# A fused attention, MoE and FFN kernel: where and in which pieces the FFN's weights are converted from 64 to 32 bits

## The chip, the cores and the metric

The kernel runs on one core of a Trainium2 chip. The metric is the device time of one execution in microseconds (us); the median of three runs is 1493.49 (1490.66 to 1493.54). Engines are named as in the profile: PE (matrix multiply, with its weight loads as PEld), DVE (vector), ACT (activation), POOL (GpSimd), SP (sync). SP, ACT and POOL each have a queue from which they issue DMA transfers; POOL's transfers are among them the indirect ones.

## The reference

```
scores = einsum('bhij,hg->bgij', q @ k^T / sqrt(64), w_pre)       # 4 batches, 12 heads, 448 rows, 64 columns
attn   = einsum('bhij,hg->bgij', softmax(scores), w_post)
x      = (attn @ v) as 1792 tokens x 768
logits = x @ w_gate; e = argmax(logits)                           # 8 experts
x      = softmax(logits)[e] * (relu(x @ w1[e]) @ w2[e])           # w1 768x1024, w2 1024x768
h      = x @ w_in; out = (h * sigmoid(h)) @ w_out                 # w_in 768x2048, w_out 2048x768
```

All inputs but w_in and w_out are 32-bit floats. Those two reach the kernel as 64-bit floats, in `wf`: 16 slices f, each 128 rows of 1536 columns (a slice of w_in beside a slice of w_out). The chip's engines see pairs of 32-bit words (low, high), and the kernel itself makes 32-bit floats of them: `high & 0xfffff`, scaled to a mantissa; `low` added to it; the sign put in; the exponent shifted out of `high`, moved to the 32-bit bias, and multiplied in. That is five DVE and two ACT instructions for a chunk, a load of D (two words a column) before and a store to `w_d[f]` in memory behind. A chunk's working buffer is CM.

## The kernel before

Products in full precision are made of three matmuls on numbers split in a high and a low part (`mm3`, L785): ACT makes the high part (a cast), DVE the low one (a subtraction).

**Attention** (to about 525 us). 16 blocks of 120 or 88 rows, each with 12 or 9 groups of 10 rows by 12 heads. A group is mixed (L787 to L789), its maximum taken (L373), exponentiated on ACT (L383), scaled, mixed again (L414), and evacuated (`a_sb`, L256). A planner (`Plan`, L147) sets the order of every instruction from priorities, costs in us written beside each operation, and rings of buffers; operations that list ACT and DVE both go to the one that it has free. Scores S go from rows to groups by SP's transfers (`relay`, L336). Each block ends with its gate on DVE (L486 to L500, seven instructions on 120x8 numbers and one exponential on ACT). Among this work the planner spreads the conversion (`convert`, L518) of the slices 0 to 3 (`FA = 4`) in 24 chunks of 256 columns.

**MoE** (to about 930 us). Tokens are sorted by expert into 18 slots of 128 rows. POOL's queue gathers a slot's rows (L849) and scatters its results y to `y_d` (L895). Per slot the weights are split (L838, L839), `mm1` makes h (L875) and `mm2` makes y (L893). From the 24th step on `Convert` (L917) converts slices 4 to 7 in 16 chunks of 384 columns: a new chunk's load (L936) and an old one's store (L958) are issued by POOL, and a step of each chunk in work is taken after each quarter slot. In the last slots ACT's queue also loads rows of `y_d` for the FFN (`xload`, L907), which waits for the scatters.

**FFN** (the rest). 80 units (gi, f): five groups of rows (four of 384, one of 256) by 16 slices; the first 40 units take slices 0 to 7 for all groups and store partial sums to `p_d`, the other 40 take slices 8 to 15 and add them. The order is that of the code: `s1` (18 matmuls, sigmoid L985, product L987, split into gh and gl), in some units the transposes of the next group (`fT`), `s2` of the unit before (18 matmuls), `fsplit` of the weights two units ahead (rhi on ACT, rlo on DVE, L844 and L845), `fload` of those four units ahead (SP, L902), and a step of the conversion of slices 8 to 15: 16 chunks of 768 columns, begun over 36 units, two buffers each of D and CM, POOL issuing. In the step k counted from the load: 1 L946, 2 L948 (ACT), 3 L950 and L951, 4 L954 (ACT), 5 L956, L957 and the store.

Of the kernel before, what the change touches and what calls it, by code (L numbers as in the profile page):

```python
# [9 lines left out]
F32 = mybir.dt.float32  # L10
# [9 lines left out]
DM = H * D  # L20
# [8 lines left out]
NS0 = 18  # L29
# [3 lines left out]
FA = 4  # L33
# [50 lines left out]
def fused_kernel(ctx: ExitStack, tc: tile.TileContext, q, k, v, w_pre, w_post, wg, w1, w2, wf, cst, out):  # L84
# [57 lines left out]
    attention(tc, nc, q, k, v, x_d, oh, cum, zsum, c_e8, ident, (wp1h, wp1l), wp2, wg_sb, wf, w_d, bias_e, bias_1)  # L142
# [86 lines left out]
def attention(tc, nc, q, k, v, x_d, oh, cum, zsum, c_e8, ident, wp1, wp2, wg_sb, wf, w_d, bias_e, bias_1):  # L229
    with ExitStack() as st:  # L230
# [16 lines left out]
        T = [tuple(one.tile([128, S], F32R, name=f"{n}{h}") for n in ("kh", "kl")) for h in range(H)]  # L247

# [221 lines left out]
        def lsum(i, part):  # L470
            def fn(e):
                m = blocks[i][2]
                if ("lg", i) not in tiles:
                    tiles["lg", i] = sm.tile([120, 2, E], F32, name="lg", tag="lg", bufs=2)
                V.reduce_sum(tiles["lg", i][:m, part, :], tiles["rows", i, part][:, :, 128:].rearrange("p j e -> p e j"),
                             axis=AX.X)
            return fn
# [8 lines left out]
        def gate(i):  # L486
            def fn(e):
                m = blocks[i][2]
                lgs = tiles.pop(("lg", i))
                mx, nm, mn = (sm.tile([120, 1], F32, name=n, tag=n, bufs=2) for n in ("lmx", "lnm", "lmn"))  # L490
                lg, cand = (sm.tile([120, E], F32, name=n, tag=n, bufs=2) for n in ("lgt", "cand"))
                V.tensor_tensor(out=lg[:m], in0=lgs[:m, 0, :], in1=lgs[:m, 1, :], op=ALU.add)
                V.reduce_max(mx[:m], lg[:m], axis=AX.X)
                V.scalar_tensor_tensor(out=cand[:m], in0=lg[:m], scalar=mx[:m], in1=c_e8[:m],
                                       op0=ALU.is_equal, op1=ALU.mult)
                V.tensor_reduce(out=mn[:m], in_=cand[:m], axis=AX.X, op=ALU.min)
                V.tensor_scalar(out=oh[:m, i, :], in0=c_e8[:m], scalar1=mn[:m], scalar2=None, op0=ALU.is_equal)
                V.tensor_tensor(out=cum[:, i + 1, :], in0=cum[:, i, :], in1=oh[:, i, :], op=ALU.add)
                V.tensor_scalar(out=nm[:m], in0=mx[:m], scalar1=-1.0, scalar2=None, op0=ALU.mult)
                tiles["lx", i] = (lg, nm)  # L500
            return fn

        def gexp(i):
            def fn(e):
                m = blocks[i][2]
                lg, nm = tiles.pop(("lx", i))
                ex = sm.tile([120, E], F32, name="ex", tag="ex", bufs=2)
                A.activation(out=ex[:m], in_=lg[:m], func=ACTF.Exp, bias=nm[:m], accum_out=zsum[:m, i:i + 1])
            return fn
# [94 lines left out]
        for i in range(NBLK):  # L604
# [18 lines left out]
            for half in range(2):  # L623
# [6 lines left out]
                add(("lsum", i, half), n + P["rows"], ((DVE, .18),), lsum(i, half), [("rows", i, half)], [],  # L630
                    [("tp", "rows", i, half)])
            add(("store", i), f, ((SP, .63),), store(i), [("rowsx", i, h) for h in range(2)], extra=3.0)
            add(("gate", i), n + P["rows"], ((DVE, 1.6),), gate(i), [("lsum", i, h) for h in range(2)] + ([("gate", i - 1)] if i else []))
            add(("gexp", i), n + P["rows"], ((ACT, .4),), gexp(i), [("gate", i)])
# [157 lines left out]
def experts(tc, nc, x_d, y_d, w1, w2, wf, w_d, p_d, bias_e, bias_1, out, ident, oh, cum, zsum, consts,  # L792
# [6 lines left out]
    with outer:  # L799
# [117 lines left out]
        class Convert:  # L917


            def __init__(self, pool, f0, f1, cols, steps):  # L920
                self.pool, self.cols = pool, cols
                self.chunks = [(f, c) for f in range(f0, f1) for c in range(0, 2 * DM, cols)]
                self.starts = [n * steps // len(self.chunks) for n in range(len(self.chunks))]
                self.time, self.begun, self.live = 0, 0, []

            def tick(self):
                for x in list(self.live):
                    x[0] += 1
                    self.step(*x)
                    if x[0] == 5:  # L930
                        self.live.remove(x)
                while self.begun < len(self.chunks) and self.starts[self.begun] <= self.time:
                    f, c = self.chunks[self.begun]
                    d = self.pool.tile([128, self.cols, 2], I32, name="D", tag="D", bufs=2)
                    m = self.pool.tile([128, self.cols], I32, name="CM", tag="CM", bufs=2)
                    nc.gpsimd.dma_start(out=d.rearrange("p a b -> p (a b)"), in_=wv[f, :, 2 * c:2 * (c + self.cols)])  # L936
                    self.live.append([0, f, c, d, m])
                    self.begun += 1
                self.time += 1

            def step(self, k, f, c, d, m):
                V, A = nc.vector, nc.scalar
                low, high = d[:, :, 0], d[:, :, 1]
                fl = m.bitcast(F32)
                if k == 1:
# [261 lines left out]
```

## Time and profile before

| | us |
|---|---|
| median of three runs | 1493.49 |
| the profiled execution | 1491.27 |
| its span, first to last instruction | 1489.0 |
| PE, DVE, ACT, POOL busy | 1346.9, 1118.9, 915.4, 144.4 |
| mean granted clock of PE | 0.963 |

Busy time is read with care: matmuls are pipelined, and a PE that is busy by this table need not be at its peak. A row of the stretches below has, in this order: start and end in us, the length, the busy time of PE, PEld, DVE, ACT and POOL (with the number of instructions), PE's granted clock, the share of time that the DMA engines were busy, and GB/s. A timeline's row has start, duration, engine, line, operation, tiles (written <- read), and in brackets the idle time before it and what ended that by the profile.

### The profile page before, as it was taken

To read this page: it belongs to the slowest core of one execution; us is meant where nothing else is said; L and a number is where in the kernel's file an instruction comes from. 1 tells how busy PE (TensorE), PEld (TensorE's weight loads), DVE (VectorE), ACT (ScalarE), POOL (GpSimd) and SP (SyncE) were. 2 spreads that over 40 slices of the span, in tenths; PEclk is the share of its full clock that TensorE was granted. 3 is DMA by queue.
4 is the path that set the end of the run, shared out by engine and by line. 5 is a ranking of instruction groups with operands and counts; after the bars stand their busy time and mean duration, and the time that the engine had idled before them with its cause. 6 is when DMAs were issued, how large, how long until landed. Compare 5 with 4: busy or idle time off the path is not lost. (4 is left out here: it accounts for less than half of the span.)

```text
span 1489.0 us, 23973 instructions
## 1 busy us (share of the span) xinstructions
PE 1346.9 (90%) x8838; PEld 1222.2 (82%) x8838; DVE 1118.9 (75%) x2022; ACT 915.4 (61%) x1574; POOL 144.4 (10%) x161
## 2 busy tenths in 40 slices
PE   4899999999999989999989888979697949999998
PEld 2787887878788878888877777979696949999997
DVE  5999899989999758888988888557475647455554
ACT  4788787868877636778886777535253525333333
POOL 4000000000000020421211211010101010001001
PEclk9999999999999989999999999989798979999999
DMA  8346545554543360594648642556556546355543
GB/s 242 137 153 174 190 141 161 172 157 149 176 158 130 76 219 22 199 382 147 217 159 306 217 141 80 190 169 212 191 169 202 183 167 223 128 191 191 176 143 138
DMA packets 105417, 259.83 MB, mean 174 GB/s; under 512 B 8956, under 2 KB 61472, under 8 KB 105296
## 3 DMA queue, kind: packets, MB, share of 16 engines
q1 hardware_dynamic: 92096, 200.57, 40.5%
q0 software_dynamic: 11184, 52.18, 10.3%
q10 hardware_dynamic: 2016, 5.51, 1.1%
q8 instruction: 72, 1.18, 0.3%
q14 instruction: 49, 0.40, 0.1%
HBM read 254.28 MB, written 36.18 MB: 195 GB/s over the span
## 5 line engine op out<-in xcount | busy, mean ns | idle before, releaser
L839 DVE TENSOR_TENSOR rlo<-wraw,rhi 128x1536 fp32r<-128x1536 f32 x144 | 246.7, 1755 | 44.8 <-ACT rhi L838 44.5
L838 ACT CAST rhi<-wraw 128x1536 fp32r<-128x1536 f32 x144 | 205.1, 1476 | 11.3 <-DMA wraw<-in_moe_w_dram 11.3
L845 DVE TENSOR_TENSOR rlo<-wf,rhi 128x1536 fp32r<-128x1536 f32 x80 | 140.5, 1758 | 67.8 <-ACT rhi L844 67.8
L414 PEld LDWEIGHTS m<-WM,E 120*112 120x112 f32 (+1 forms) x1440 | 168.5, 177 | 24.8 <-issue 6.3
L414 PE MATMUL m<-WM,E 120*112 120x120 f32 (+1 forms) x1440 | 178.0, 268 | 9.4 <-DVE WM L403 7.5
L787 PE MATMUL b<-fxhi,rhi 128*128 128x384 f32 (+1 forms) x480 | 160.9, 335 | 26.8 <-DVE sg L987 23.4
L787 PE MATMUL b<-rhi,gh 128*128 128x384 f32 x436 | 153.0, 351 | 24.7 <-ACT gh L844 23.9
L789 PE MATMUL b<-fxhi,rlo 128*128 128x384 f32 (+1 forms) x480 | 159.4, 332 | 1.4 <-DVE rlo L845 1.4
L788 PE MATMUL b<-fxlo,rhi 128*128 128x384 f32 (+1 forms) x480 | 159.3, 332 | 0.0
L789 PE MATMUL b<-rhi,gl 128*128 128x384 f32 x436 | 150.7, 346 | 0.0
L788 PE MATMUL b<-rlo,gh 128*128 128x384 f32 x436 | 150.7, 346 | 0.0
L985 ACT ACTIVATE sg<-b 128x384 f32<-128x384 f32 (+1 forms) x80 | 37.5, 469 | 164.4 <-PE b L789 164.1
L844 ACT CAST gh<-sg 128x384 fp32r<-128x384 f32 (+1 forms) x77 | 38.1, 495 | 154.8 <-DVE sg L987 154.8
L383 ACT ACTIVATE E<-m,mx 120x448 f32<-120x448 f32 x180 | 113.9, 634 | 24.8 <-DVE mx L373 13.1
L844 ACT CAST rhi<-wf 128x1536 fp32r<-128x1536 f32 x80 | 118.1, 1478 | 3.5 <-issue 2.2
L787 PEld LDWEIGHTS b<-fxhi,rhi 128*128 128x128 f32 x480 | 93.5, 195 | 29.4 <-DVE sg L987 25.6
L373 DVE TENSOR_REDUCE mx<-m 120x1 f32<-120x448 f32 x180 | 110.4, 617 | 4.2 <-PE m L789 2.8
L357 DVE TENSOR_TENSOR GL<-G,GH 120x448 fp32r<-120x448 f32 x180 | 109.8, 616 | 0.3
L787 PEld LDWEIGHTS b<-rhi,gh 128*128 128x128 f32 x436 | 84.9, 195 | 26.2 <-ACT gh L844 24.8
L323 PE MATMUL qkp<-kh,qs 128*120 128x448 f32 (+1 forms) x192 | 83.6, 436 | 23.3 <-DVE qs L314 20.4
L256 ACT CAST GH<-G 120x448 fp32r<-120x448 f32 (+1 forms) x151 | 85.1, 565 | 31.5 <-PE m L789 14.3
L789 PE MATMUL b<-rhi,hlo 128*128 128x384 f32 x288 | 97.7, 339 | 1.7 <-DVE hlo L845 1.7
(192 smaller groups left out, 3092.7 us busy)
## 6 DMA issues: line engine op xcount, KB each, us to landing
wraw<-in_moe_w_dram SPq DMA_DIRECT2D x76, 1536.0 KB
wf<-w_d SPq DMA_DIRECT2D x80, 768.0 KB
G<-S SPq DMA_DIRECT2D x176, 210.0 KB
D<-in_wf_dram POOLq DMA_DIRECT2D x16, 768.0 KB, 5.6
rawq<-in_q_dram SPq DMA_DIRECT2D x32, 360.0 KB
raw<-in_k_dram SPq DMA_DIRECT2D x36, 224.0 KB
D<-in_wf_dram SPq DMA_DIRECT2D x24, 256.0 KB
D<-in_wf_dram POOLq DMA_DIRECT2D x16, 384.0 KB, 3.6
```

Of the source, the lines that this page charges most:

```text
L256: (A.copy if eng == "act" else V.tensor_copy)(out, in_)
L357: V.tensor_tensor(out=t[:n], in0=x[:n], in1=hi[:n].bitcast(F32), op=ALU.subtract)
L373: V.tensor_reduce(out=mx[:n], in_=tiles["m1", i, g][:n, :S], axis=AX.X, op=ALU.max, negate=True)
L383: A.activation(out=t[:n], in_=tiles.pop(("m1", i, g))[:n, :S], func=ACTF.Exp, bias=tiles.pop(("mx", i, g))[:n], accum_out=tiles["z", i, g ...
L414: nc.tensor.matmul(p[:, c, :, :nr], x[:n, c * CH:(c + 1) * CH], wm[:n, :, :nr], start=True, stop=True)
L787: nc.tensor.matmul(p, lh, rh, start=first, stop=False)
L788: nc.tensor.matmul(p, lh, rl, start=False, stop=False)
L789: nc.tensor.matmul(p, ll, rh, start=False, stop=last)
L838: nc.scalar.copy(hi, src)
L839: nc.vector.tensor_tensor(out=lo, in0=src, in1=hi.bitcast(F32), op=ALU.subtract)
L844: nc.scalar.copy(hi, src)
L845: nc.vector.tensor_tensor(out=lo, in0=src, in1=hi.bitcast(F32), op=ALU.subtract)
```

## The change

Slices 0 to 7 are converted in the attention (48 chunks of 256 columns), none in the MoE, and 8 to 15 in the FFN in 24 chunks of 512 columns. There a chunk has three buffers of D and CM, a tile CE for the exponent, its steps in units 2 to 5 after its load, and SP issues the load ahead of the unit's `fload`. The gates of four blocks are computed together, from sums kept in `lgs`; the logits have their maximum subtracted on DVE, and the exponentials are summed there. A copy of the partial sums goes from DVE to ACT.

```
-FA = 4
+        lgs = one.tile([120, 4, 2, E], F32, name="lgs")
         def lsum(i, part):
-                V.reduce_sum(tiles["lg", i][:m, part, :], ...)
+                V.reduce_sum(lgs[:m, i % 4, part, :], ...)
-        def gate(i):            # 7 DVE instructions on [120, 8], each block
+        def gate(b):
+                V.tensor_tensor(out=lg, in0=lgs[:, :, 0, :], in1=lgs[:, :, 1, :], op=ALU.add)
+                V.tensor_reduce(out=mx, in_=lg, axis=AX.X, op=ALU.max)
+                V.tensor_tensor(out=lg, in0=lg, in1=wide(mx), op=ALU.subtract)
+                V.scalar_tensor_tensor(out=cand, in0=lg, scalar=0.0, in1=ce, op0=ALU.is_equal, op1=ALU.mult)
+                V.tensor_reduce(out=mn, in_=cand, axis=AX.X, op=ALU.min)
+                V.tensor_tensor(out=cand, in0=ce, in1=wide(mn), op=ALU.is_equal)
+                V.tensor_tensor(out=oh[:, w], in0=cand, in1=wide(c_val[:120, w]), op=ALU.mult)
+                for i in range(4 * b, 4 * b + 4):
+                    V.tensor_tensor(out=cum[:, i + 1, :], in0=cum[:, i, :], in1=oh[:, i, :], op=ALU.add)
+        def gexp(b):  ...  A.activation(out=tiles["ex", b], in_=tiles.pop(("lx", b)), func=ACTF.Exp)
+        def zadd(b):  ...  V.reduce_sum(zsum[:, 4 * b:4 * b + 4], tiles.pop(("ex", b)), axis=AX.X)
-        for f in range(FA):
+        for f in range(FH):
-        class Convert: ...
+        CC = 512
+        chunks = [(f, c) for f in range(FH, NF) for c in range(0, 2 * DM, CC)]
+        def conv_load(n, steps):
+            while len(live) < len(chunks) and len(live) * steps // len(chunks) <= n:
+                d = gpool.tile([128, CC, 2], I32, name="D", tag="D", bufs=3)
+                nc.sync.dma_start(out=d.rearrange("p a b -> p (a b)"), in_=wv[f, :, 2 * c:2 * (c + CC)])
+                live.append([n, f, c, d, None, None])
+        def conv_step(n):
+                if k == 2:
+                    m = x[4] = gpool.tile([128, CC], I32, name="CM", tag="CM", bufs=3)
+                    e = x[5] = gpool.tile([128, CC], I32, name="CE", tag="CE")
+                    V.tensor_scalar(out=m, in0=high, scalar1=0xfffff, ...)
+                    V.tensor_scalar(out=e, in0=high, scalar1=20, scalar2=0x7ff, ...)
+                elif k == 3:            # ACT: mantissa of m, exponent of e
+                elif k == 4:            # DVE: low added, sign put in (the last reads of D)
+                elif k == 5:
+                    V.tensor_tensor(out=fl, in0=fl, in1=e.bitcast(F32), op=ALU.mult)
+                    nc.gpsimd.dma_start(out=w_d[f][:, c:c + CC], in_=fl)
-                        nc.vector.tensor_copy(ob[:, 384:], acc[2 * j + 1][:, :384])
+                        nc.scalar.copy(ob[:, 384:], acc[2 * j + 1][:, :384])
-            conv = Convert(wr, FA, FH, 384, 4 * NS0 - 30)
-            slots(0, NS0, hook, tick)
+            slots(0, NS0, hook)
-            conv = Convert(gpool, FH, NF, DM, len(work) // 2 - 4)
+                conv_load(n, len(work) // 2 - 4)
                 if n + 4 < len(work):
                     fload(n + 4)
-                conv.tick()
+                conv_step(n)
```

DVE in the FFN from the end of unit 5 (units counted from 0), before; the number behind CM and D tells chunks apart:

```order
L845 TENSOR_TENSOR rlo_11910<-wf_11793,rhi_11909 128x1536
L956 TENSOR_TENSOR CM_11612<-CM_11612,D_11611 128x768
L957 SCALAR_TENSOR_TENSOR CM_11612<-D_11611,CM_11612 128x768
L950 SCALAR_TENSOR_TENSOR CM_11737<-D_11736,CM_11737 128x768
L951 TENSOR_SCALAR D_11736<-D_11736 128x768
L946 TENSOR_SCALAR CM_11857<-D_11856 128x768
L987 TENSOR_TENSOR sg_11940<-b1_11921,sg_11940 128x384
L845 TENSOR_TENSOR gl_11944<-sg_11940,gh_11943 128x384
L845 TENSOR_TENSOR fxlo1_11641<-b0_11947,fxhi1_11640 128x3x128
```

The same place after (L956 is the multiplication now, L944 and L945 the AND and the shift, L986 the sigmoid product):

```order
L852 TENSOR_TENSOR rlo_11838<-wf_11717,rhi_11837 128x1536
L956 TENSOR_TENSOR CM_11657<-CM_11657,CE_11658 128x512
L952 SCALAR_TENSOR_TENSOR CM_11721<-D_11597,CM_11721 128x512
L953 SCALAR_TENSOR_TENSOR CM_11721<-D_11597,CM_11721 128x512
L944 TENSOR_SCALAR CM_11847<-D_11715 128x512
L945 TENSOR_SCALAR CE_11848<-D_11715 128x512
L986 TENSOR_TENSOR sg_11870<-b1_11851,sg_11870 128x384
L852 TENSOR_TENSOR gl_11874<-sg_11870,gh_11873 128x384
L852 TENSOR_TENSOR fxlo1_11562<-b0_11877,fxhi1_11561 128x3x128
L852 TENSOR_TENSOR rlo_11902<-wf_11781,rhi_11901 128x1536
L956 TENSOR_TENSOR CM_11721<-CM_11721,CE_11722 128x512
L944 TENSOR_SCALAR CM_11913<-D_11779 128x512
```

Before, the first step of chunk CM_11857 stands directly behind the last steps of CM_11612, whose buffer it takes, and ahead of the next sigmoid product. After, CM_11847 has a buffer of its own, and that of CM_11657 is first written again, as CM_11913, one unit later than its multiplication.

POOL's queue in the middle of the MoE, before:

```order
L895 DMA y_d_61<-y_9182,idx_s_102 1792x768
L936 DMA D_9342<-in_wf_dram 128x768
L849 DMA xg_9345<-x_d_60,idx_g_101 128x768
L958 DMA w_d5_67<-CM_9180 128x384
L936 DMA D_9428<-in_wf_dram 128x768
L895 DMA y_d_61<-y_9379,idx_s_102 1792x768
L849 DMA xg_9544<-x_d_60,idx_g_101 128x768
L958 DMA w_d5_67<-CM_9343 128x384
L936 DMA D_9581<-in_wf_dram 128x768
L958 DMA w_d5_67<-CM_9429 128x384
L895 DMA y_d_61<-y_9584,idx_s_102 1792x768
```

and after (L856 is the gather, L902 the scatter):

```order
L902 DMA y_d_61<-y_8105,idx_s_102 1792x768
L856 DMA xg_8257<-x_d_60,idx_g_101 128x768
L902 DMA y_d_61<-y_8289,idx_s_102 1792x768
L856 DMA xg_8469<-x_d_60,idx_g_101 128x768
L902 DMA y_d_61<-y_8501,idx_s_102 1792x768
L856 DMA xg_8653<-x_d_60,idx_g_101 128x768
L902 DMA y_d_61<-y_8685,idx_s_102 1792x768
L856 DMA xg_8837<-x_d_60,idx_g_101 128x768
```

The conversion's loads and stores, which stood between scatters and gathers, are gone.

SP's queue in the first half of the FFN, before:

```order
L902 DMA wf_12355<-w_d0_62 128x1536
L902 DMA wf_12414<-w_d1_63 128x1536
L902 DMA wf_12475<-w_d2_64 128x1536
L902 DMA wf_12537<-w_d3_65 128x1536
L902 DMA wf_12604<-w_d4_66 128x1536
L902 DMA wf_12674<-w_d5_67 128x1536
```

and after (L909 is the weights' load):

```order
L909 DMA wf_11717<-w_d7_69 128x1536
L932 DMA D_11779<-in_wf_dram 128x1024
L909 DMA wf_11781<-w_d0_62 128x1536
L909 DMA wf_11841<-w_d1_63 128x1536
L932 DMA D_11905<-in_wf_dram 128x1024
L909 DMA wf_11907<-w_d2_64 128x1536
L932 DMA D_11971<-in_wf_dram 128x1024
L909 DMA wf_11973<-w_d3_65 128x1536
L909 DMA wf_12039<-w_d4_66 128x1536
```

Loads of D now stand between the loads of the weights, two for every three.

Over the whole attention the planner's order gives DVE 53 copies of a_sb instead of 64, 59 of S instead of 65, 41 casts instead of 44, and 31 copies of xT and xb instead of 26; ACT has the others.

## Rows read from the trace of the kernel before

**Rows 1.** Five stretches: busy PE, PEld, DVE, ACT, POOL, then clock, DMA.
```profile
100.00:500.00 400.00, 383.60 (x3315) 328.39 (x3313) 373.24 (x1022) 313.89 (x751) 0.00 (x0) 1.00 0.50 158
660.00:765.00 105.00, 100.19 (x527) 88.39 (x526) 95.39 (x95) 88.94 (x102) 23.54 (x24) 1.00 0.58 195
765.00:930.00 165.00, 142.93 (x716) 123.96 (x715) 135.76 (x141) 118.85 (x137) 28.79 (x32) 0.94 0.53 184
930.00:1249.00 319.00, 264.33 (x1464) 258.84 (x1464) 186.99 (x234) 133.15 (x186) 24.36 (x44) 0.90 0.55 185
1249.00:1489.00 240.00, 233.08 (x1386) 232.27 (x1384) 124.61 (x149) 92.14 (x121) 17.20 (x16) 1.00 0.48 169
```
**Rows 2.** DVE's waits, 930 to 1249 us: in total, times, longest.
```profile
DVE CM L946 <- DMA w_d<-CM: 51.3, 8, 10.8
...
DVE CM L946 <- DMA D<-in_wf_dram: 6.9, 6, 1.3
```
**Rows 3.** PE's waits in the same stretch.
```profile
PE b L787 <- ACT gh L844: 23.9, 4, 12.9
PE b L787 <- DVE sg L987: 23.4, 5, 10.0
```
**Rows 4.** Timeline of DVE in one unit of that stretch.
```profile
1116.18 0.56 DVE L987 TENSOR_TENSOR sg<-b,sg 128x384 f32<-128x384 f32 x1 [0.34 <-ACT sg L985]
1117.32 0.56 DVE L845 TENSOR_TENSOR gl<-sg,gh 128x384 fp32r<-128x384 f32 x1 [0.58 <-ACT gh L844]
1119.18 1.76 DVE L845 TENSOR_TENSOR rlo<-wf,rhi 128x1536 fp32r<-128x1536 f32 x1 [1.30 <-ACT rhi L844]
...
1129.57 0.56 DVE L946 TENSOR_SCALAR CM<-D 128x768 int32<-128x768 int32 x1 [5.30 <-DMA w_d<-CM]
```
**Rows 5.** Groups by form there: busy us, mean ns, idle before.
```profile
L950 DVE SCALAR_TENSOR_TENSOR CM<-D,CM 128x768 f32<-128x768 uint32 x16 | 15.2, 951 | 0.0
L951 DVE TENSOR_SCALAR D<-D 128x768 int32<-128x768 int32 x16 | 9.0, 561 | 0.6
```
**Rows 6.** Timeline of DVE in the attention, 271 to 279 us.
```profile
271.62 0.29 DVE L532 TENSOR_SCALAR CM<-D 128x256 int32<-128x256 int32 x1
271.82 0.65 DVE L256 COPY a_sb<-m 112x480 f32<-112x480 f32 x1
...
276.31 0.41 DVE L538 SCALAR_TENSOR_TENSOR CM<-D,CM 128x256 int32<-128x256 int32 x1
276.63 0.28 DVE L403 TENSOR_SCALAR WM<-wp,rz 120x120 f32<-120x120 f32 x1
...
277.63 0.14 DVE L492 TENSOR_TENSOR lgt<-lg 120x8 f32<-120x8 f32 x1
...
278.88 0.27 DVE L403 TENSOR_SCALAR WM<-wp,rz 120x120 f32<-120x120 f32 x1
```
**Rows 7.** A group of ACT in the attention, by form.
```profile
L534 ACT ACTIVATE CM<-CM,bias 128x256 f32<-128x256 int32 x19 | 9.6, 507 | 0.7 <-DVE CM L532 0.6
```
**Rows 8.** Timeline of ACT late in the MoE.
```profile
778.41 0.56 ACT L893 ACTIVATE y<-b,gate_s 128x384 f32<-128x384 f32 x1
...
790.00 0.34 ACTq L907 DMA_DIRECT2D x<-y_d  x1
790.39 0.60 ACT L875 ACTIVATE h<-b 128x512 f32<-128x512 f32 x1 [8.20 <-PE b L788]
```
**Rows 9.** Timeline of POOL at the same time.
```profile
783.48 0.55 POOL L958 DMA_DIRECT2D w_d<-CM  x1 [12.43 <-DVE CM L957]
784.33 1.42 POOL L895 DMA_INDIRECT y_d<-y,idx_s  x1 [0.30 <-issue]
```
**Rows 10.** ACT's waits, 765 to 930 us.
```profile
ACT h L875 <- DMA y_d<-y,idx_s: 14.5, 2, 7.8
```
**Rows 11.** Transfers: queue, count, KB each, us from issue to landing.
```profile
D<-in_wf_dram POOLq DMA_DIRECT2D x16, 768.0 KB, 5.6
...
w_d<-CM POOLq DMA_DIRECT2D x16, 384.0 KB, 3.1
```

More of the change, by code (lines that the diff above doesn't have):

```diff
@@ L141, in fused_kernel @@
         nc.vector.tensor_tensor(out=wp1l, in0=wp1, in1=wp1h.bitcast(F32), op=ALU.subtract)
-    attention(tc, nc, q, k, v, x_d, oh, cum, zsum, c_e8, ident, (wp1h, wp1l), wp2, wg_sb, wf, w_d, bias_e, bias_1)
+    attention(tc, nc, q, k, v, x_d, oh, cum, zsum, c_e8, c_val, ident, (wp1h, wp1l), wp2, wg_sb, wf, w_d, bias_e, bias_1)
     experts(tc, nc, x_d, y_d, w1, w2, wf, w_d, p_d, bias_e, bias_1, out, ident, oh, cum, zsum,
@@ L226, in order, with attention @@
         return result
-def attention(tc, nc, q, k, v, x_d, oh, cum, zsum, c_e8, ident, wp1, wp2, wg_sb, wf, w_d, bias_e, bias_1):
+def attention(tc, nc, q, k, v, x_d, oh, cum, zsum, c_e8, c_val, ident, wp1, wp2, wg_sb, wf, w_d, bias_e, bias_1):
     with ExitStack() as st:
@@ L472, in fn @@
                 m = blocks[i][2]
-                if ("lg", i) not in tiles:
-                    tiles["lg", i] = sm.tile([120, 2, E], F32, name="lg", tag="lg", bufs=2)
-                V.reduce_sum(tiles["lg", i][:m, part, :], tiles["rows", i, part][:, :, 128:].rearrange("p j e -> p e j"),
+                V.reduce_sum(lgs[:m, i % 4, part, :], tiles["rows", i, part][:, :, 128:].rearrange("p j e -> p e j"),
                              axis=AX.X)
@@ L484, in store @@
             return fn
-        def gate(i):
+        def gate(b):
             def fn(e):
[L488 to L500, printed above, removed]
+                w = slice(4 * b, 4 * b + 4)
+                mx, mn = (sm.tile([120, 4], F32, name=n, tag=n, bufs=2) for n in ("lmx", "lmn"))
+                lg, cand = (sm.tile([120, 4, E], F32, name=n, tag=n, bufs=2) for n in ("lgt", "cand"))
+                wide = lambda x: x.unsqueeze(2).to_broadcast([120, 4, E])
+                ce = c_e8[:120].unsqueeze(1).to_broadcast([120, 4, E])
+                V.tensor_tensor(out=lg, in0=lgs[:, :, 0, :], in1=lgs[:, :, 1, :], op=ALU.add)
[7 more added lines that the diff above has]
+                    V.tensor_tensor(out=cum[:, i + 1, :], in0=cum[:, i, :], in1=oh[:, i, :], op=ALU.add)
+                tiles["lx", b] = lg
@@ L501, in gate, with gexp @@
             return fn
-        def gexp(i):
+        def gexp(b):
             def fn(e):
[L505 to L508, printed above, removed]
+                tiles["ex", b] = sm.tile([120, 4, E], F32, name="ex", tag="ex", bufs=2)
+                A.activation(out=tiles["ex", b], in_=tiles.pop(("lx", b)), func=ACTF.Exp)
+            return fn
@@ L629, in attention @@
                     [("rows", i, half)] + ([("store", i - 1)] if i else []), [], [("tp", "rows", i, half)])
-                add(("lsum", i, half), n + P["rows"], ((DVE, .18),), lsum(i, half), [("rows", i, half)], [],
+                add(("lsum", i, half), n + P["rows"], ((DVE, .18),), lsum(i, half), [("rows", i, half)] + ([("gate", b - 1)] if b and t == 0 else []), [],
                     [("tp", "rows", i, half)])
             add(("store", i), f, ((SP, .63),), store(i), [("rowsx", i, h) for h in range(2)], extra=3.0)
-            add(("gate", i), n + P["rows"], ((DVE, 1.6),), gate(i), [("lsum", i, h) for h in range(2)] + ([("gate", i - 1)] if i else []))
-            add(("gexp", i), n + P["rows"], ((ACT, .4),), gexp(i), [("gate", i)])
+            if t == 3:
+                add(("gate", b), n + P["rows"], ((DVE, 2.6),), gate(b), [("lsum", j, h) for j in range(4 * b, i + 1) for h in range(2)])
+                add(("gexp", b), n + P["rows"], ((ACT, .3),), gexp(b), [("gate", b)])
+                add(("zadd", b), n + P["rows"], ((DVE, .2),), zadd(b), [("gexp", b)])
         for j in range(12):
@@ L915, in experts @@
         wv = wf.bitcast(I32)
[L917 to L942, printed above, removed]
@@ L957, in step @@
                     V.scalar_tensor_tensor(out=m, in0=high, scalar=-(1 << 31), in1=m, op0=ALU.bitwise_and, op1=ALU.bitwise_or)
-                    nc.gpsimd.dma_start(out=w_d[f][:, c:c + self.cols], in_=fl)
+                elif k == 5:
+                    fl = m.bitcast(F32)
+                    V.tensor_tensor(out=fl, in0=fl, in1=e.bitcast(F32), op=ALU.mult)
+                    nc.gpsimd.dma_start(out=w_d[f][:, c:c + CC], in_=fl)
         def fT(gi, j, hf, kind="p1"):
@@ L1114, in hook @@
                     xload(1, j - 4)
-            conv = Convert(wr, FA, FH, 384, 4 * NS0 - 30)
-            def tick(n):
-                if n >= 24:
-                    conv.tick()
-            slots(0, NS0, hook, tick)
-            assert not conv.live and conv.begun == len(conv.chunks)
+            slots(0, NS0, hook)
             total = nc.values_load(es_i[0:1, 2 * NS:2 * NS + 1], min_val=0, max_val=NS)
```

29 lines of the change are left out of this document (16 added, 13 removed).

## The prediction

> **What bounds the kernel now.** I read four views in this order: busy time by stretch, the waits of DVE and PE in the first half of the FFN, a timeline of DVE there, and timelines of ACT and POOL late in the MoE.
>
> The stretches show three different limits [rows 1]. In the attention (100 to 500 us) DVE is busy for 373 of 400 us and ACT for 314, at full clock; PE's 384 us are pipelined matmuls that overlap, so DVE is the fullest engine there. Late in the MoE (765 to 930 us) PE is idle for 165 - 142.9 = 22.1 us, while from 660 to 765 us it is idle for 4.8 of 105. The two halves of the FFN have the same 40 units of matmuls each, yet the first takes 319 us and the second 240. The first half alone converts weights.
>
> There DVE stands at L946, the first step of a chunk's conversion, for 51.3 us until the store of an older chunk has left the buffer CM, and for 6.9 us until D is loaded [rows 2]. DVE takes its instructions in order, so the sigmoid product L987 stands behind L946, and PE waits for what follows: 23.9 us for gh and 23.4 us for sg [rows 3]. The timeline shows it once: rlo, the rest of an older chunk, then L946 after 5.30 us of idling [rows 4]. The granted clock of the stretch is 0.90 against 1.00 in the second half [rows 1]: part of the matmuls between such stalls ran at 1.2 instead of 2.4 GHz.
>
> **FFN.** Before, two buffers of 768 columns serve chunks that start every 2.25 units, and a chunk's store is issued in its 5th unit; the chunk two later wants the buffer in that same unit or the next: the wait is built into the order. After, three buffers of 512 columns serve chunks that start every 1.5 units. CM is taken in a chunk's second unit and stored in its fifth, so the next user comes a whole unit after the store. A store of 384 KB landed 3.1 us after its issue [rows 11]; the new one is 256 KB and a unit is about 6.4 us (240 us over 32 full units and 8 of two thirds, 37.3 in all) [rows 1]. I take the waits at L946 as gone. D is free after the fourth step now, because the exponent lies in CE, so a load is issued at least one unit ahead of its use.
>
> What is late next? The floor by PE is the second half's 240 us, plus the first half's 78 more instructions (mostly transposes) at 233.1/1386 = 0.17 us, 13 us [rows 1]: 253 us, 66 less than now. DVE is the other candidate. From L987 to gl is 1.14 us and from gl to rlo 1.86 us (waits for ACT included), and rlo takes 1.76 us [rows 4]: 4.76 us a unit. The conversion of a 768-column chunk costs 3 x 0.951 + 2 x 0.561 = 3.98 us [rows 5]. L538 shows about 0.41 us for 256 columns [rows 6], so three times the columns cost 2.3 times the time and about 0.14 us of each instruction is fixed. Sixteen chunks cost 63.6 us; 24 smaller ones of the same total width add 8 x 5 x 0.14 = 5.6: 69 us, 1.73 us a unit. DVE then needs 6.5 us a full unit, as much as PE, and an estimated 6.0 us in the eight 256-row units (three operations are shorter by some 0.13 us, and ACT's casts as well), where PE alone would need 4.3: 32 x 6.5 + 8 x 6.0 + 5 for the start = 261 us. I take -58 us. The bounds: -66 at PE's floor; and -44 if the uneven load (every third unit holds steps of three chunks, some 1.1 us above the mean, 13 times) isn't smoothed over. The 14 copies of partial sums that go from DVE to ACT (three at a group's end) I cost at nothing: ACT is busy for 133 of 319 us [rows 1]; without that cover they cost their own time at most, some 0.5 us each, 7 us.
>
> **MoE.** All 16 chunks leave it. PE loses no work. What it gains is POOL's queue: y of a slot was ready at 778.41 + 0.56 us, but its scatter L895 stood behind a conversion's store, which waited 12.43 us for DVE, and began at 784.33 [rows 8, 9]. On ACT's queue L907 loads rows of y_d and waits for that scatter until 790.00, so h, behind it, came after 8.20 us of idling; the row names PE, but it is L907 that stands in front [rows 8]. Two more such waits add 14.5 us [rows 10]. Without the store ahead of it the scatter starts some 0.3 us after y [rows 9], 5.1 us earlier, and each of the three waits shrinks to about 3 us: 22.7 - 9 = 13.7 us. By PE it is 22.1 us of idling less the 4.6% of the stretch before (7.5 us), 14.6 us [rows 1]. I take -13; the bounds are 0 (the gap is filled by another wait) and -20 (the idling nearly gone).
>
> The Trainium skill, "DMA: Bandwidth & Descriptors", section "Issuing engines are not separate DMA queues", says that issuing from several engines saves only the time of issue, which is usually small beside the transfer. Taken by itself it would price the cleared POOL queue at almost nothing and the sum would be 13 us higher. The trace speaks against it here: what the store's issue cost was 12.43 us of waiting, not issue [rows 9].
>
> **Attention.** It takes 24 chunks more. In place, start to next start, an AND or shift on 256 columns costs 0.20 us and a three-operand step 0.32 [rows 6]: 2 x 0.20 + 3 x 0.32 = 1.36 us a chunk, 33 us on DVE, and two activations of about 0.51 us on ACT [rows 7], 24 us. A gate now takes 1.25 us from its first instruction to the next engine work, 16 times: 20 us [rows 6]. The four new ones have 8 wide instructions and 4 additions to cum each; at 0.18 us (a seventh of 1.25) and some more for 32 columns that is 2.4 us, 9.5 in all: -10.5. The planner, seeing more DVE work, hands ACT 11 copies of a_sb at 0.65 us [rows 6], six of S and three casts, and takes back five others: about -8. DVE gains 33 - 10.5 - 8 = +14 us net, ACT some +27. ACT has 86 us to spare in 400 and DVE 27 [rows 1], so DVE sets the price: at its present fullness 14/0.93 = 15 us, with some of it in present gaps. I take +14. The bounds are -10 (the new order happens to close a third of the 27 us) and +35 (the relief by ACT comes to nothing: the 33 us at full price, and 2 more). SP's queue carries 48 transfers more (24 loads, 24 stores) between the relays of S; no row prices what a relay loses behind one of them, and I leave it inside these bounds: 0 while DVE is the fullest engine, 10 us (0.2 us each, an estimate from the 0.34 us that ACT takes to issue one [rows 8]) if each is felt. The last gate now stands behind one block's sums with four additions in a row: +1 us at the hand-over.
>
> **Sum.** -58 - 13 + 14 + 1 = -56 us. The profiled execution took 1491.27 us (span 1489.0), 2.2 below the median of the three runs, 1493.49. 1491.27 - 56 = 1435; on the scale of the median 1437 us.
>
> **Rivals.** (1) Attention saturates: both DVE and ACT slow each other, and it grows by 35 instead of 14 us: 1458. For it: DVE at 93%. Against: the gates get cheaper.
>
> (2) The cleared POOL queue is worth nothing, because the waits of ACT on y_d go to another place: 1450. For it: the scatter itself still has to land before L907. Against it: the 5.1 us by which one scatter was late [rows 8, 9]. It is also what the rule of "DMA: Bandwidth & Descriptors" in the Trainium skill, cited above, comes to.
>
> (3) The wait for CM stays, so the change doesn't do what it says. The stores stay on POOL's queue. If they land 8 us after issue instead of 3.1 [rows 11], each of 21 reuses costs 8 - 6.5 = 1.5 us: +31, 1468. For it: waits up to 5.3 us after the last step [rows 4].
> The Trainium skill, "SBUF — State Buffer", section "SBUF: two separate sides", says that GpSimd can't write the descriptors of its DMAs while DVE runs in a mode that uses both ports, and that DMAs of SP and ACT escape this. By that rule the loads are cured and the stores are not. The trace bears it out in part only: stores were waited for 51.3 us and loads 6.9, both from POOL [rows 2], but two buffers explain the difference as well.
>
> (4) Slower: SP's queue. From the fourth on, 21 loads of D stand on SP until DVE has read the old D, and the weight load wf behind each is held as well. If the two land one after the other, D (512 KB) and wf (768 KB) take 5.6 x 5/3 = 9.3 us at the rate of the 768 KB load [rows 11]; wf is wanted about one unit and 2 us later, after 8.5 us. Every us above 8.5 costs up to 21 us; the gain of 56 is gone from 2.7 us on, at 11.2 us from release to landing. At 12 us it is 21 x 3.5 = 74: 1511. Against: DMA engines are busy for 55% in this stretch [rows 1], and transfers overlap.
>
> **How the numbers follow.** Chances: forecast 0.66 (its own range 1420 to 1450), rival 1 0.14, rival 2 0.08, rival 3 0.07, rival 4 0.05. All but rival 4 and the edges of 1 and 3 are faster than before by over 0.2%, about what a measurement can tell from no change: faster 0.93, same 0.02, slower 0.05. The range from 1415 (attention at 0, FFN at -66, MoE at -13) to 1462 takes in rivals 1 and 2.
>
> **What would show it.** Right: L946's successor (L944) waits for no store; the first FFN half takes about 260 us with a granted clock near 1.00; its DVE is over 80% busy; the scatters start 0.3 us after y; the attention ends some 14 us later. Wrong: rhi waits for wf (rival 4); DVE still idles at L944 for w_d (rival 3); the MoE is as long as before (rival 2); attention over 30 us longer (rival 1).

## The result, and the profile after

The changed kernel takes 1428.88 us (median of four runs, 1426.94 to 1430.43) against 1492.76 for the kernel before on the same chip: a ratio of 0.957, 95% interval 0.956 to 0.959. The profiled execution took 1429.51 us, its span is 1427.7, PE's mean clock 0.981 (0.963 before).

I cut both traces at the same events: attention to the issue of the last store of x_d, MoE from there to the first sigmoid of the FFN, then 40 units, 40 units, and the rest.

| us | before | after | difference | forecast |
|---|---|---|---|---|
| attention | 525.9 | 540.3 | +14.4 | +14 |
| MoE (its first 1.9 us of the difference are the hand-over) | 408.8 | 390.6 | -18.2 | -13 + 1 |
| FFN, first half | 314.7 | 252.8 | -61.9 | -58 |
| FFN, second half | 226.7 | 226.7 | 0 | 0 |
| rest | 12.9 | 17.2 | +4.3 | 0 |
| span | 1489.0 | 1427.7 | -61.3 | -56 |

The stretches of the profile after, with the columns of [rows 1]:

```profile
100.00:514.00 414.00, 392.14 (x3327) 328.85 (x3327) 390.91 (x1064) 334.30 (x784) 0.00 (x0) 0.99 0.56 174
600.00:760.00 160.00, 156.44 (x834) 139.22 (x833) 134.97 (x109) 125.11 (x133) 39.96 (x22) 1.00 0.60 210
760.00:930.00 170.00, 159.10 (x820) 140.88 (x819) 130.18 (x102) 123.79 (x135) 21.12 (x14) 0.96 0.47 162
930.00:1184.00 254.00, 246.01 (x1457) 240.53 (x1457) 179.72 (x261) 140.10 (x215) 19.02 (x35) 1.00 0.62 227
1184.00:1427.00 243.00, 232.15 (x1380) 231.21 (x1379) 124.02 (x148) 92.23 (x122) 18.86 (x17) 0.99 0.48 167
```

The first FFN half (930 to 1184) now runs at full clock and PE is idle for 8 us of 254. Of the 65 us between this stretch and the 319 us of [rows 1], 46.7 are idle time of PE, and 18.3 are its busy time, for nearly the same matmuls (1464 recorded before, 1457 after) at a granted clock of 1.00 instead of 0.90. DVE's and PE's waits there answer to [rows 2, 3]:

```profile
DVE rlo L852 <- ACT rhi L851: 44.3, 40, 3.2
DVE gl L852 <- ACT gh L851: 22.3, 40, 0.6
DVE sg L986 <- ACT sg L984: 8.8, 7, 4.1
DVE CM L944 <- DMA w_d<-CM: 0.5, 1, 0.5
```
```profile
PE b L794 <- ACT gh L851: 3.1, 3, 1.2
PE b L796 <- DVE rlo L852: 2.6, 6, 0.5
PE b L794 <- DVE sg L986: 2.3, 4, 0.9
```

Of 51.3 us of waiting for stores 0.5 are left, and none for loads. What remains on DVE are waits for ACT, 75.4 us in all and 4.1 us at most; with its 179.7 us of busy time they fill the stretch. One full unit, from rlo to rlo, where [rows 4] has the 5.30 us gap (start, duration, engine, line, operation, tiles, idle before):

```profile
1045.33 1.76 DVE L852 TENSOR_TENSOR rlo<-wf,rhi 128x1536 fp32r<-128x1536 f32 x1 [0.73 <-ACT rhi L851]
1047.01 0.69 DVE L956 TENSOR_TENSOR CM<-CM,CE 128x512 f32<-128x512 f32 x1
1047.61 0.69 DVE L952 SCALAR_TENSOR_TENSOR CM<-D,CM 128x512 f32<-128x512 uint32 x1
1048.33 0.69 DVE L953 SCALAR_TENSOR_TENSOR CM<-D,CM 128x512 int32<-128x512 int32 x1
1048.94 0.42 DVE L944 TENSOR_SCALAR CM<-D 128x512 int32<-128x512 int32 x1
1049.27 0.42 DVE L945 TENSOR_SCALAR CE<-D 128x512 int32<-128x512 int32 x1
1049.61 0.55 DVE L986 TENSOR_TENSOR sg<-b,sg 128x384 f32<-128x384 f32 x1
1050.74 0.56 DVE L852 TENSOR_TENSOR gl<-sg,gh 128x384 fp32r<-128x384 f32 x1 [0.58 <-ACT gh L851]
1051.21 0.55 DVE L852 TENSOR_TENSOR fxlo<-b,fxhi 128x384 fp32r<-128x384 f32 x1
1052.50 1.76 DVE L852 TENSOR_TENSOR rlo<-wf,rhi 128x1536 fp32r<-128x1536 f32 x1 [0.73 <-ACT rhi L851]
```

Even a unit with the steps of three chunks (L956; L952 and L953; L944 and L945) goes through without a gap: 7.2 us, and the next, lighter one is shorter. The instructions have the sizes that were worked out from [rows 5]: 0.69 and 0.42 us for 512 columns, 2.9 us a chunk.

Late in the MoE, ACT and POOL, answering to [rows 8 to 10]:

```profile
788.76 0.58 ACT L900 ACTIVATE y<-b,gate_s 128x384 f32<-128x384 f32 x1 [0.73 <-PE b L796]
...
797.28 0.34 ACTq L914 DMA_DIRECT2D x<-y_d  x1
797.67 0.60 ACT L882 ACTIVATE h<-b 128x512 f32<-128x512 f32 x1 [5.10 <-DMA y_d<-y,idx_s]
```
```profile
789.62 1.01 POOL L902 DMA_INDIRECT y_d<-y,idx_s  x1 [15.05 <-ACT y L900]
```
```profile
ACT h L882 <- DMA y_d<-y,idx_s: 10.4, 2, 5.3
```

The scatter starts 0.3 us after y is ready, 5 us sooner than before, as forecast. But it lands only 7.6 us after its issue (at 797.2), and ACT, which stands at L914 until then, still idles for 5.1 us.

### The profile page after: what moved, and what is told of

The parts are those of the page before. It is cut to its first block, busy times and chain, and to the rows that moved or that the text cites. A ratio compares the mean times of both kernels' runs of the same rounds, so it can differ in the third digit from the quotient of the medians.

```text
span 1427.7 us, 24068 instructions
## 1 busy us (share of the span) xinstructions
PE 1336.1 (94%) x8838; PEld 1204.5 (84%) x8838; DVE 1097.9 (77%) x2010; ACT 927.7 (65%) x1607; POOL 126.7 (9%) x121
## 5 line engine op out<-in xcount | busy, mean ns | idle before, releaser
L845 ACT CAST rhi<-wraw 128x1536 fp32r<-128x1536 f32 x144 | 205.0, 1476 | 11.6 <-DMA wraw<-in_moe_w_dram 11.5
L794 PE MATMUL b<-fxhi,rhi 128*128 128x384 f32 (+1 forms) x480 | 157.5, 328 | 5.5 <-ACT rhi L851 3.2
L794 PE MATMUL b<-rhi,gh 128*128 128x384 f32 x436 | 149.3, 342 | 3.1 <-ACT gh L851 3.1
L796 PE MATMUL b<-rhi,gl 128*128 128x384 f32 x436 | 147.6, 338 | 0.0
L795 PE MATMUL b<-rlo,gh 128*128 128x384 f32 x436 | 146.7, 336 | 0.0
L258 ACT CAST GH<-G 120x448 fp32r<-120x448 f32 (+1 forms) x153 | 86.0, 564 | 23.5 <-DMA G<-S 12.5
L794 PE MATMUL b<-rhi,hhi 128*128 128x384 f32 x288 | 99.2, 344 | 0.0
L795 PE MATMUL b<-rlo,hhi 128*128 128x384 f32 x288 | 97.6, 339 | 0.0
```

What stands on the lines that cost most here:

```text
L258: (A.copy if eng == "act" else V.tensor_copy)(out, in_)
L794: nc.tensor.matmul(p, lh, rh, start=first, stop=False)
L795: nc.tensor.matmul(p, lh, rl, start=False, stop=False)
L796: nc.tensor.matmul(p, ll, rh, start=False, stop=last)
L845: nc.scalar.copy(hi, src)
```

## The experiments

Where a stage is named, it is cut as in the table above. DVE's waits are those of 930 to 1250 us.

**Two CM buffers.** `name="CM", tag="CM", bufs=3)` becomes `bufs=2)` in the kernel after.

> The kernel after, with two buffers of CM in the FFN instead of three; all else, the loads on SP among it, stays. Theory A (the wait for a store's landing was built into the order, and the third buffer takes it out): the chunk two later now takes CM in the unit in which the store is issued, so DVE idles at L944 for w_d, some 22 times for 2 to 3 us; the first FFN half goes from 253 to 290 us or more, the whole to about 1470 us. Rival (moving the loads from POOL to SP, or smaller chunks, cured it): no change, 1429 us, and no wait at L944 for w_d.

1493.17 us, ratio to before 0.999 (0.998 to 1.001): all of the gain is gone. First half 318.0, 65 us longer than after, other stages as after. DVE waits at L944 for 64.1 us in 22 waits; for eleven of them the profile names the store, for the others it names no releaser ("issue"):

```profile
DVE CM L944 <- issue: 33.1, 11, 4.7
DVE CM L944 <- DMA w_d<-CM: 31.0, 11, 5.5
```

**Three buffers and 512 columns alone**, in the kernel before, with its old steps and POOL's loads:

```
-            conv = Convert(gpool, FH, NF, DM, len(work) // 2 - 4)
+            conv = Convert(gpool, FH, NF, 512, len(work) // 2 - 4, 3)     # 3 buffers each of D and CM
```

> The kernel before, with the FFN's conversion in 24 chunks of 512 columns and three buffers each of D and CM, and nothing else: five steps in the old order, exponent in D, POOL issuing. Theory A (what counts is the time from a store's issue to the next use of its buffer): three chunks now start within 4.5 units as two did, CM is still taken in a chunk's first unit and stored in its fifth, so the wait stays; first FFN half 300 us or more, whole 1475 us or more. Rival (a third buffer by itself cures it): first half about 253 us, whole 1432 us.

1507.08 us, slower than before: 1.010 (1.009 to 1.012); first half 327.9.

```profile
DVE CM L947 <- DMA w_d<-CM: 74.9, 11, 9.2
```

So the third buffer is needed (cm2) and gains nothing with the old steps. With the old steps CM is taken in unit 1 of a chunk and stored in unit 5, while every second chunk three later starts 4 units after: eleven times the AND still stands in the unit of the store, right behind it.

**The moment at which CM is taken**, alone, in the kernel after:

```
-                if k == 2:
+                if k == 1:
                     m = x[4] = gpool.tile([128, CC], I32, name="CM", tag="CM", bufs=3)
-                    e = x[5] = gpool.tile([128, CC], I32, name="CE", tag="CE")
                     V.tensor_scalar(out=m, in0=high, scalar1=0xfffff, ...)
+                elif k == 2:
+                    e = x[5] = gpool.tile([128, CC], I32, name="CE", tag="CE")
```

> The kernel after, with only the moment changed at which a chunk takes its buffer CM: its AND stands in the chunk's first unit instead of the second (three buffers of 512 columns, the separate exponent tile CE and loads on SP stay). The store is issued in the fifth unit as after; the chunk three later starts 4 or 5 units after and wants the buffer 0 or 1 unit after the store instead of 1 or 2. Theory A, the time between a store's issue and the buffer's next use is what counts: the first FFN half takes 300 to 325 us instead of 252.8, and the AND waits for the store for 25 us or more in all. Rival, the separate exponent tile is what counts (the other edits of the chunk's steps do little): 253 to 262 us, waits under 5 us.

1459.01 us, 0.975 (0.972 to 0.979); first half 282.4. The wait is back eleven times, but each is about 0.4 of ffn3's:

```profile
DVE CM L943 <- DMA w_d<-CM: 28.6, 11, 5.4
```

The half is 29.6 us longer: 18 short of theory A's range, 20 above the rival's, with the waits that A named (28.6 us). So the moment is a cause, but not of everything in ffn3. It left open why ffn3 waits 6.8 us a time and this kernel 2.6. The trace has it in the landing of the stores: 5.0 us in ffn3 (median of the five that the trace has), 2.6 here. In ffn3 the next D is loaded by POOL 0.5 us ahead of the stores that are waited for, because the same instruction (the last of unit 5) reads D and finishes CM. Two more runs asked which of the two matters, the queue or the moment.

**ffn3 with D loaded by SP:**

```
-                    nc.gpsimd.dma_start(out=d.rearrange(...), in_=wv[...])
+                    (nc.sync if self.bufs == 3 else nc.gpsimd).dma_start(out=d.rearrange(...), in_=wv[...])
```

> The kernel before with chunks of 512 columns and three buffers (as the run named ffn3), with the FFN's loads of D on SP instead of POOL. In ffn3 the load of the next D and the store of CM are released by the same instruction, the load is issued 0.5 us ahead of the store on POOL, and the store lands 5.0 us after its issue; in early_cm, whose loads are on SP, it lands after 2.6 us. Theory A, the store's data stand behind the load's on POOL's transfers: without the load the store lands after 2.6 to 3 us, each of the 11 recorded waits shrinks by 4 us, and the first FFN half takes 280 to 295 us instead of 327.9. Rival, the order of the chunk's steps costs it (two more instructions in front of the store, D held to the end): the store lands sooner but the half stays at 310 to 328 us. Second rival: D's loads now wait on SP in front of the loads of wf and hold them: rhi waits for wf, 320 us or more.

1490.32 us, 0.998 (0.997 to 1.000); first half 314.7. Theory A fell: POOL carries only stores there now, and they land after 5.3 us all the same. The half is where the rival had it, but the stores do not land sooner, as it also had it.

```profile
DVE CM L947 <- DMA w_d<-CM: 63.4, 11, 6.6
```

The times of issue show why. SP's load is released at the same moment as the store, and a load of wf goes out behind it, so the store's 256 KB share the DMA engines with 512 and 768 KB of loads:

```profile
1045.60 0.33 SPq L937 DMA_DIRECT2D D<-in_wf_dram  x1
1045.98 0.42 SPq L902 DMA_DIRECT2D wf<-w_d  x1
```
```profile
1045.83 0.54 POOL L959 DMA_DIRECT2D w_d<-CM  x1 [12.37 <-DVE CM L958]
```

The Trainium skill, "DMA: Bandwidth & Descriptors", section "Issuing engines are not separate DMA queues", has this: transfers interleave on the same DMA engines, whichever engine issued them. The trace agrees (5.3 against 5.0 us). The second rival (wf held up on SP) shows no wait of rhi for wf.

**early_cm with D loaded by POOL** (`nc.sync.dma_start` becomes `nc.gpsimd.dma_start` for D):

> early_cm with the FFN's loads of D on POOL instead of SP. D is free a step before the store here, so its load is issued a unit ahead of the store, not right in front of it. Theory A, only a load right in front of a store delays it: the stores land after 2.6 to 3.5 us and the first FFN half takes 278 to 290 us, as early_cm's 282.4. Rival, any load on POOL slows the stores there: they land after 4.5 us or more and the half takes 305 to 328 us.

1466.37 us, 0.983 (0.981 to 0.985); first half 296.3, between the two theories. The stores land after 4.6 us (median), but the loads of D are not the reason: the stores with a load of D 1.3 us behind them land after 4.65 us (median of 7), those without one after 4.6 (12). What stands close to every store here is a load of wf, which SP issues 0.87 us ahead of it (SP, then POOL, then that store's size and landing):

```profile
996.05 0.32 SPq L909 DMA_DIRECT2D wf<-w_d  x1
```
```profile
996.93 0.54 POOL L958 DMA_DIRECT2D w_d<-CM  x1 [8.79 <-DVE CM L957]
```
```profile
w_d<-CM POOLq DMA_DIRECT2D x1, 256.0 KB, 4.7
```

In early_cm SP holds that load behind the one of D until D is free, so that the two go out 1.1 and 1.5 us behind a store or 5 us ahead of it:

```profile
1014.90 0.54 POOL L958 DMA_DIRECT2D w_d<-CM  x1 [12.55 <-DVE CM L957]
```
```profile
1015.97 0.33 SPq L932 DMA_DIRECT2D D<-in_wf_dram  x1
1016.39 0.41 SPq L909 DMA_DIRECT2D wf<-w_d  x1
```
```profile
w_d<-CM POOLq DMA_DIRECT2D x1, 256.0 KB, 2.3
```

When its last D is loaded, wf stands 0.87 us ahead of the store in early_cm too, and the two landings recorded there are 6.7 and 4.3 us. The stores that land late are thus those with a load issued shortly ahead of them, whichever tile it loads and whichever queue it is on. The stores of 256 KB in the first half, those apart that come within 6 us behind the stores of `p_d` or the loads of x:

| the load next ahead of the store | it lands after (median) | in |
|---|---|---|
| none within 3 us | 2.5 us (44 stores) | after, cm2, early_cm |
| wf, 1.6 us | 3.3 to 3.9 (4) | ffn3, ffn3_sp |
| wf, 0.87 us | 4.6 (47) | early_cm_pool, pool_loads, the last of the three above |
| D, 0.2 to 0.5 us | 5.3 (20) | ffn3_sp, ffn3 |

**D loaded by POOL in the kernel after** (the same edit, CM taken late):

> The kernel after, with the FFN's loads of D issued by POOL instead of SP. Theory A (what counts is when a buffer comes free, not which queue issues): stores stand behind a load that waits for DVE, but have one unit of slack; 1429 to 1434 us. Rival (transfers issued by POOL are late beside DVE's work, as loads and stores were before): DVE waits for D at L944 for 1 us or more in each of 24 chunks; the first FFN half 270 us or more, the whole 1445 us or more.

1423.00 us, 0.953 (0.951 to 0.954); first half 251.9. The stores land after 4.6 us here as well (wf is again 0.87 us ahead of each), yet DVE has no wait for them: with CM taken a unit later a store has the time. SP is no part of the gain. Of the 6 us that this kernel is faster 4.8 lie in the last stage (12.4 instead of 17.2, below); the MoE's 1.8 (388.8) are within what it varies by from run to run.

The Trainium skill, "SBUF — State Buffer", section "SBUF: two separate sides", says that descriptors of POOL's DMAs can't be written while DVE is in a mode of two ports, and advises SP or ACT. No wait of this pair of kernels bears it out here: 251.9 us with POOL's loads, 252.8 with SP's. Which of DVE's operations here run in such a mode no run shows.

**MoE: the queue or the work?** Slices 4 to 7 go back into the MoE (the kernel after otherwise), with POOL issuing the conversion's DMAs as before, and the same with SP:

```
-        for f in range(FH):            # attention's list
+        for f in range(4):
+        conv = Convert(wr, 4, FH, 384, 4 * NS0 - 30)      # ticked from the 24th step on
```

> The kernel after, with slices 4 to 7 converted in the MoE again, in 16 chunks of 384 columns, loads and stores on POOL as before the change; the attention converts slices 0 to 3. The FFN and the joint gates stay as after. Theory A: the attention loses the 33 us of DVE work and what the planner gave back for it, and ends about 24 us earlier than after, 10 us earlier than before the change (the gates); the MoE is 18 us longer again, with ACT held for the scatters; about 1423 us. Rival (the joint gates are worth nothing): the attention ends as before the change, 14 us earlier than after; 1433 us.

1431.60 us, 0.957 (0.956 to 0.959); attention 528.7, MoE 412.2.

> As moe_pool, but SP issues the MoE's conversion loads and stores. Theory A (the MoE gained because POOL's scatters no longer stand behind stores that wait for DVE): scatters start 0.3 us after y, and the MoE is only some 6 us longer than after (DVE's and ACT's own work); about 1411 us. Rival (the MoE gained by DVE's and ACT's work that left it): as long as in moe_pool, 18 us longer than after, about 1423 us. Possible loss on the way: weight loads stand behind the conversion's on SP, which would show as ACT waiting for wraw.

1430.71 us, 0.956 (0.954 to 0.959); attention 530.0, MoE 405.2. One early slot, the fifth, varies from run to run whatever the edit (22.6, 24.2 and 21.0 us in moe_pool, moe_sp and after), so the comparison is made behind it, from the end of its y to the first sigmoid:

| MoE behind the fifth slot | us |
|---|---|
| as before: before, ffn3, ffn3_sp, moe_pool | 274.3, 273.9, 274.1, 274.0 |
| conversion's DMAs on SP: moe_sp | 265.9 |
| no conversion: after; cm2, early_cm, old_gate; pool_loads, early_cm_pool | 254.3; 252.8, 254.4, 254.3; 250.3, 250.6 |

So of the 19.7 us from moe_pool to after the queue is worth 8.1, and 11.6 is left that only the absence of the conversion gives. With its DMAs on SP ACT hardly waits for scatters any more, 3.8 us instead of 27.5 (moe_pool's rows first, then moe_sp's):

```profile
ACT h L882 <- DMA y_d<-y,idx_s: 23.3, 3, 8.2
ACT y L900 <- DMA y_d<-y,idx_s: 4.2, 1, 4.2
```
```profile
ACT D L961 <- DMA y_d<-y,idx_s: 2.3, 1, 2.3
ACT CM L955 <- DMA y_d<-y,idx_s: 1.5, 1, 1.5
```

These 23.7 us less of waiting gave only 8.1 us of time. moe_sp's PE is idle for 18.7 of the 170 us from 760 on, after's for 10.9:

```profile
760.00:930.00 170.00, 151.32 (x780) 133.88 (x778) 146.14 (x154) 130.95 (x152) 18.66 (x14) 0.96 0.57 193
```

Two of PE's waits there are those for low parts that DVE makes late, being busy with the conversion; moe_pool has them as well (6.7 and 3.5 us), and after, the same two take 2.6 and 1.0 us:

```profile
PE b L795 <- DVE rlo L846: 7.8, 4, 3.7
PE b L796 <- DVE xlo L852: 3.8, 4, 1.6
```

DVE's wait for loads of D is longer with SP than in moe_pool (6.8 us there), so the queue may be worth more than 8.1 us:

```profile
DVE CM L953 <- DMA D<-in_wf_dram: 12.0, 4, 4.0
```

**The old gates**, one block at a time, in the kernel after:

> The kernel after, with one gate for each block as before the change. Theory A (the sum of the prediction: joint gates take 10 us off DVE, which sets the attention's pace): the attention ends 10 us later, at 550 us, whole 1439 us. Rival (from moe_pool, where the attention with joint gates and the old conversion ended 3 us later than before the change: the gates give nothing, since the planner fills DVE either way, and four additions and a wider gate stand at the end): 3 us earlier, at 537 us, whole 1426 us.

1438.32 us, 0.964 (0.962 to 0.966); attention 549.8, MoE 392.0. The joint gates are worth 9.5 us there (the profiled execution is 3.6 us above the median of its kernel; a second pair, best1 and best2 below, has 11.2). But in moe_pool and moe_sp, with joint gates and the conversion of before, the attention is 2.8 and 4.1 us *longer* than before, where ffn3 and ffn3_sp, unchanged there, have 526.4 and 523.8. The gates' DVE time did shrink: a wide instruction takes 0.19 us and serves four blocks,

```profile
L495 DVE TENSOR_TENSOR lgt<-lgt,lmx 120x32 f32<-120x32 f32 x3 | 0.6, 192 | 0.1
L501 DVE TENSOR_TENSOR cum<-cum,oh 120x8 f32<-120x8 f32 x12 | 2.0, 167 | 0.4
```

so eight of them and four additions make 2.2 us for four blocks instead of 5.0. Why that gives nothing beside half of the conversion is not shown. DVE is nearly as full there as before, 369.9 of 400 us against 373.2; but the granted clock of this stretch is 0.98 in both kernels, against 1.00, 0.99 and 1.00 in before, ffn3 and ffn3_sp, which alone could make the difference. The stretch in moe_pool:

```profile
100.00:500.00 400.00, 386.29 (x3300) 331.03 (x3299) 369.93 (x977) 302.19 (x706) 0.00 (x0) 0.98 0.51 157
```

**x loaded by POOL.** The six early loads of x that stand on ACT's queue in the MoE go to POOL's, behind the scatters that they wait for:

```
-                    xload(0, j)                   # nc.scalar
+                    xload(0, j, nc.gpsimd)        # and xload(1, j - 4, nc.gpsimd)
```

> The kernel after, with the six loads of y_d during the MoE issued by POOL, behind the scatters, instead of ACT. Theory A (in the kernel after, ACT still stands at these loads until a scatter has landed, up to 7.6 us, and that lengthens slots 10 to 13): ACT's h waits for no scatter, the slots of 24.6 and 22.7 us come down to about 19, the MoE is 8 to 10 us shorter, whole about 1420 us. Rival (these slots are long because of the FFN's transposes and splits that are put into them): the same length, 1429 us.

1422.47 us, 0.955 (0.953 to 0.956); MoE 380.9, 9.7 less. ACT has no wait for y_d left, and the slots of 24.6 and 22.7 us take 18.8 and 19.5.

**Together.** x on POOL, D on POOL and the old gates:

> The kernel after with three edits: one gate for each block, the FFN's loads of D issued by POOL, the loads of y_d in the MoE issued by POOL. If the parts add up (loads -6, gates -3, loads of y_d -8): about 1412 us. If the edits meet on POOL's queue (the loads of y_d hold gathers and scatters up): no better than pool_loads, 1423 us.

1423.94 us, 0.954 (0.953 to 0.956): MoE 382.8, but attention 553.4. The old gates, put at 3 us of gain there, cost 11.2 us of the attention against the next kernel. With the joint gates (the text says seven loads; there are six):

> The kernel after, with two other queues: the loads of D in the FFN on POOL, and the seven early loads of x (the rows of y_d for the first two groups) on POOL instead of ACT. Theory A, the parts add up: attention 540 us as after, MoE 381 as with the x loads alone on POOL, first FFN half 252, second 227, tail 12.5 as with the D loads alone on POOL: a span of 1412.5 us and a time of 1414 to 1417 us, 0.948 to 0.950 of the kernel before. Rival: the gain of the x loads on POOL is chance in where the scatters land, and does not come a second time: MoE 389 to 391, 1421 to 1424 us.

1415.88 us (1415.18 to 1417.31), 0.947 (0.945 to 0.950), the fastest here: attention 542.2, MoE 379.9, FFN 252.0 and 226.8, rest 12.5. The parts add up.

## Why the prediction was right, point by point

**FFN, first half: right, and cut a little short** (-61.9 for -58). The wait for CM was the cause, and the order of a store and the buffer's next use is what cured it. The working took three buffers, the later taking of CM and the early release of D as one; the runs divide the first two, and the release of D was tested only together with the rest of the new steps. Each is needed: without the third buffer 65 us come back, without the later taking 29.6, and with the old steps 32.3 more (314.7 in ffn3_sp, 282.4 in early_cm), of which the slower landing accounts for up to 30 us (11 waits by 5.3 - 2.6 us; in early_cm_pool a landing later by 2.0 us cost 13.9). That last price was not in the text, which used one landing time of 3.1 us for all stores; they take 2.3 to 5.3 us by what was issued shortly ahead.

What was wrong here is DVE's demand of 6.5 us a unit as the limit. Its 4.76 us from L987 to the end of rlo hold 1.9 us of waits for ACT (0.58 and 1.30, [rows 4]); the text says that they are in it, and yet calls for a DVE that is busy for over 80%. It is busy for 179.7 of 254 us, 71%. Units of 384 rows do take 6.46 us in the mean, but PE sets that pace: it is idle for 8 us in all, and its floor, 253 us, was reached. That 6.5 came out is luck. Units of 256 rows take 5.75 instead of 6.0. The 319 us that the forecast starts from hold 4.7 us ahead of the first sigmoid; without these, and without its 5 us for the start, it was 314.3 to 256, and 314.7 to 252.8 came.

**MoE: more than forecast, the reason half right** (-18.2; -20.1 without the hand-over, at the bound of -20 and not at -13). The scatters start 5 us sooner, as forecast, and ACT's three waits of 22.7 us shrank to 10.4 (two remain, because the scatter of 789.62 took 7.6 us to land), where 9 was forecast. The step that failed is to take these waits at their full length as the gain, and all else as nothing ("PE loses no work. What it gains is POOL's queue"). Left out was that the conversion's own steps keep DVE from the low parts that PE waits for. The runs give 8.1 us to the queue and 11.6 to the work; that the total came near is in part that one term was too large and the other missing. Where the conversion is gone the waits do count nearly in full: in xload_pool the last 10.4 us of them bring 9.7. Rival 2 had the MoE as long as before and is refuted, but the queue alone was not worth 13 us.

**Attention: right in size, in part by luck** (+14.4; +14 was the forecast). DVE's busy time, 373.2 of 400 us before and 390.9 of 414 after, grew by 17.7. The three terms are not independent, though: the gates' -10.5 is 9.5 to 11.2 beside the full conversion and nothing (+2.8 and +4.1) beside half of it. The conversion of 24 more chunks costs 11.6 us with the joint gates (540.3 - 528.7) and 23.9 with the old ones (549.8 - 525.9). How the planner's choices make this difference, and what part of it is the clock, wasn't settled. The hand-over cost 1.9 us for 1.

**Rivals 1, 3 and 4** did not come: attention stayed under +35, no store was waited for beyond 0.5 us, and rhi never waited for wf. The loads of wf are held on SP behind those of D, as rival 4 had it, but what this changed is that the stores land sooner (2.6 us in after, 4.6 in pool_loads). DMA engines were busy for 62% of the first half.

**Not seen: the end of the kernel**, +4.3 us. The long one of the three DRAINs, at which POOL stands before the kernel ends, takes longer. The rows of line L1203 of before and L1194 of after (durations in ns, shortest, median and longest):

```profile
L1203 POOLq DRAIN  x3: 46/109/4607, 1483.6 to 1488.8; - x3
```
```profile
L1194 POOLq DRAIN  x3: 46/109/8869, 1418.0 to 1427.5; - x3
```

Without that the kernel would be at about 1424.6, an estimate. The sum came as close as it did partly by this: FFN and MoE with the hand-over gained 3.9 and 6.2 us more than forecast, and the end took 4.3 back.

## What to carry to other kernels

A ring of buffers waits by the distance between the step that frees a buffer and the step that takes it again: count both in the order of the code, and check the store's landing against that distance, with the loads that are issued shortly ahead of it on any queue. Here a third buffer gained nothing with the old steps (first half 327.9 and 314.7 us, before 314.7), and 65 us with the new ones. A load that waits for a transfer belongs on the queue of that transfer, not in front of an engine's computing.

## What was not expected of the hardware

POOL's long DRAIN took 8.87 us in the five kernels in whose traces POOL issues 93 transfers (after, cm2, moe_sp, old_gate, early_cm) and 9.36 with 99 (xload_pool), but 3.95 with 117 (pool_loads, early_cm_pool) and from there up to 5.26 with 149 (ffn3). Within either group it grows by 0.08 or 0.04 us a transfer; what makes the step between them is open. The row of pool_loads:

```profile
L1194 POOLq DRAIN  x3: 46/109/3953, 1416.1 to 1420.7; - x3
```

Scatters of the same size take 2.4 to 8.6 us to land (median 4.2, 18 of them, after); what decides it is open.
